# One attention-and-expert kernel, its 850 operations put in another order

## The chip, the cores and the metric

One core of one Trainium2 chip runs the whole program. The metric is the device time of one execution, in microseconds (us). The engines are TensorE (PE; its weight loads are PEld), VectorE (DVE), ScalarE (ACT), GpSimd (POOL) and SyncE (SP). All large transfers here are issued by SP, in the order of its list.

## The reference

The input x is 4 batches of 11,456 rows of 128 floats; there are 32 inducing vectors, a gate of 8 experts, and per expert two matrices (128 x 1024 and 1024 x 128). Cut to what matters:

```
h   = softmax(scale * I @ x.T) @ x             # per batch, 32 rows of 128
y   = softmax(scale * x @ h.T) @ h             # one row per row of x
e   = argmax(y @ w_gate);  g = softmax(y @ w_gate)[e]
out = g * (max(y @ w1[e], 0) @ w2[e])          # the row's own expert
```

Every row of y is a weighted mean of the 32 rows of h. Where all 32 agree on the expert and on the signs of its hidden units, the expert is linear for the whole batch, and out is the row's 32 weights times a 32 x 128 table. The kernel builds that table per batch, checks with margins that it holds for every row, counts the rows for which it does not, and runs a general path for those (none here).

## The kernel before

The 11,456 rows of a batch are cut into 6 pieces, 24 in all (k = 0 to 23; batch b has pieces 6b to 6b+5). A piece is 960 KB. It stays in SBUF from its load to its last use, and there are 19 buffers of that size ("big") for the pieces as loaded, for their transposes, and for the output. So a load has to wait until a buffer is free, and a store frees one.

Each line of `make_plan` is one operation, with a name that the text below uses:

- LT k loads piece k with the 128 features on the partitions. TR k.n turns it on PE and TE k.n evicts the turned part (ACT or DVE); for 10 of the 24 pieces a second load, LN k, brings the turned form instead.
- First pass: S1 k (scores against the inducing vectors, line 680), M1 (maximum, line 683), MQ/FD/NB (maximum over both pieces of a pair), E1 (exponential on ACT, line 720), T1 (transposition on DVE, line 723), H k (weighted sum on PE, line 733), AC.
- Per batch: hT, hn, hc (h, normed and centred), cg and ix (which expert), GA and GB (SP reads the expert's row number, then loads its weights, lines 792 and 793), G, GT, GS, GL, P, PC, PF, h4 (the table), dx to ts (the margins).
- Second pass: S2 k (scores against h, line 680 with hc), M2, N2, E2 (line 915). Four pieces make a round: LG, LV, LS, PR, C, CT compute the gate's factor. Then per piece SP (spread, line 975), W (line 978), four X k.q (line 982), four evictions V k.q (line 699 on ACT, 701 on DVE), and OUT k, the store (line 674).

The same program text, `schedule`, sets the order. It is a planner that runs when the kernel is built: each operation has a rank (a sum of four numbers of `PLAN`), a duration on the engines that may run it, and the operations that it needs. At each moment a free engine takes the ready operation of lowest rank for which a buffer is free. The planner models transfers (`Lines`: rate, restart after a pause), TensorE's row tiles and a price for a change of shape. What comes out is one fixed list per engine; on the chip each engine runs its own list in order, and waits by semaphores. Evictions named in `PLAN["ACT"]` or `PLAN["DVE"]` are bound to that engine; the others go where the planner finds room, and DVE leaves such an eviction to ACT when ACT's list is no more than `BEHIND` ns long.

Of the kernel before, what the change touches and what calls it, by code (L numbers as in the profile page):

```python
# [1324 lines left out]
```

## Time and profile before

| | |
|---|---|
| time, median of 3 runs | 173.77 us (173.07 to 175.04) |
| profiled execution | 174.46 us, its span 172.7 us |
| PE busy | 147.7 us (86% of the span) |
| DVE busy | 132.4 us (77%) |
| ACT busy | 89.8 us (52%) |
| POOL busy | 15.1 us (9%) |
| DMA moved | 61.89 MB, mean 358 GB/s |
| chain that ended last | PE 54%, DMA 30%, DVE 4%, issue 3%, ACT 2% |

Busy time of an engine is the union of its instructions; consecutive DVE and ACT instructions overlap a little in the records, so the sum of durations is larger. A wait is read from the idle time before an instruction and what ended it. Waits on SP are waits of the transfer list: everything behind the waiting transfer waits too.

### The profile page before, as it was taken

The numbers are of one execution on the slowest core, as the hardware profiler recorded it, in microseconds if no ns is written. First come the engines' busy times: TensorE is split into PE (matmuls) and PEld (weight loads), VectorE is DVE, ScalarE is ACT, GpSimd is POOL, SyncE is SP. The second block draws the span as 40 slices with busy tenths as digits, with TensorE's granted clock in tenths as the row PEclk, the third lists the DMA queues.
The fourth block names the chain that finished last, engine by engine and source line by source line (L and its number), as shares of the span: only waits on it lengthen the run. The fifth ranks groups of instructions, "written<-read, shape, count | busy, mean of one in ns | idle before, by whom it ended". The sixth has DMA issues, their size and how long they took to land.

```text
span 172.7 us, 5018 instructions
## 1 busy us (share of the span) xinstructions
PE 147.7 (86%) x1994; PEld 82.0 (48%) x1995; DVE 132.4 (77%) x367; ACT 89.8 (52%) x183; POOL 15.1 (9%) x78
## 2 busy tenths in 40 slices
PE   7799989699999999968998969799999999979000
PEld 4283648585358575637626623135533433325000
DVE  0167978157999899995998969979999999999400
ACT  3141726063674452534086543968397999657000
POOL 0100000000101000220201032000212001120000
PEclk9999999999999999999999999999999999999855
DMA  5999999999999992999995999759767999999991
GB/s 161 419 427 427 422 427 428 416 417 417 413 424 423 388 391 67 390 390 400 352 377 174 331 401 386 234 233 388 294 258 260 390 428 425 420 425 429 418 414 59
DMA packets 9679, 61.89 MB, mean 358 GB/s; under 512 B 1072, under 2 KB 1200, under 8 KB 9648
## 3 DMA queue, kind: packets, MB, share of 16 engines
q1 hardware_dynamic: 9504, 61.29, 88.7%
q8 instruction: 18, 0.29, 0.7%
q10 hardware_dynamic: 144, 0.20, 0.4%
q14 instruction: 13, 0.11, 0.2%
HBM read 37.89 MB, written 23.59 MB: 356 GB/s over the span
## 4 chain that ended last, share of the span: by engine, by line
PE 54%; DMA 30%; DVE 4%; issue 3%; ACT 2%; SPq 0%; DVEq 0%
DMA big<-in_xT 16%; PE bank L680 14%; PE bank L982 12%; PE bank L733 9%; PE bank L691 8%; DMA big<-in_xn 4%; PE bank L975 4%; DMA wt<-in_w 4%; DMA csb<-in_consts 3%; DMA out<-big 3%; DVE big L701 2%; PE bank L919 2%; PE bank L644 2%; ACT big L699 2%; PE bank L820 1%
## 5 line engine op out<-in xcount | busy, mean ns | idle before, releaser
L699 ACT COPY big<-bank 128x480 f32<-128x480 f32 (+2 forms) x110 | 55.2, 574 | 38.6 <-PE bank L691 21.9
L982 PE MATMUL bank<-mid,h 32*128 32x480 f32 x192 | 30.9, 607 | 0.9 <-DVE mid L978 0.7
L701 DVE COPY big<-bank 128x512 f32<-128x512 f32 (+2 forms) x42 | 26.1, 646 | 4.5 <-PE bank L691 4.2
L680 PE MATMUL bank<-big,csb 128*32 128x480 f32 x192 | 24.3, 570 | 4.0 <-DMA big<-in_xT 2.7
L733 PE MATMUL bank<-big,mid 128*32 128x129 f32 x720 | 24.2, 274 | 3.5 <-DMA big<-in_xn 2.2
L691 PE MATMUL bank<-csb,big 128*128 128x128 f32 x210 | 25.9, 277 | 0.4 <-DMA big<-in_xT 0.4
L733 PEld LDWEIGHTS bank<-big,mid 128*32 128x32 f32 x720 | 21.7, 110 | 9.5 <-issue 4.4
L691 PEld LDWEIGHTS bank<-csb,big 128*128 128x128 f32 x210 | 22.6, 141 | 7.2 <-issue 2.2
L683 DVE TENSOR_REDUCE mx<-bank 128x1 f32<-128x480 f32 x24 | 15.5, 647 | 11.7 <-PE bank L680 11.3
L680 PE MATMUL bank<-big,hc 128*32 128x480 f32 x192 | 22.7, 571 | 0.0
L915 ACT ACTIVATE mid<-bank,nb 128x480 f32<-128x480 f32 x24 | 15.8, 676 | 12.5 <-DVE nb L910 10.7
L720 ACT ACTIVATE mid<-bank,mx 128x480 f32<-128x480 f32 x24 | 15.2, 661 | 11.3 <-DVE mx L717 11.1
L982 PEld LDWEIGHTS bank<-mid,h 32*128 32x128 f32 x192 | 12.7, 183 | 14.5 <-ACT big L699 4.7
L906 DVE TENSOR_REDUCE mx<-bank 128x1 f32<-128x480 f32 x24 | 15.2, 639 | 0.5 <-PE bank L680 0.5
L723 DVE STREAM_TRANSPOSE mid<-mid 128x480 f32<-128x480 f32 x24 | 15.5, 660 | 0.0
L978 DVE TENSOR_TENSOR mid<-mid,bank 128x480 f32<-128x480 f32 x24 | 14.8, 639 | 0.6 <-PE bank L975 0.5
L975 PE MATMUL bank<-mid,sel 32*128 32x480 f32 x48 | 14.5, 603 | 0.5 <-DVE mid L971 0.5
L680 PEld LDWEIGHTS bank<-big,csb 128*32 128x32 f32 x192 | 5.8, 109 | 10.5 <-issue 5.9
L680 PEld LDWEIGHTS bank<-big,hc 128*32 128x32 f32 x192 | 5.2, 109 | 8.8 <-ACT big L699 4.3
L975 PEld LDWEIGHTS bank<-mid,sel 32*128 32x128 f32 x48 | 4.6, 183 | 5.1 <-ACT big L699 2.2
L919 PE MATMUL bank<-mid,gzb 128*32 128x480 f32 x48 | 6.0, 574 | 0.0
L902 POOL COPY thr_all<-thr 32x1 f32<-32x1 f32 x24 | 4.3, 177 | 19.5 <-DVE thr L895 18.7
(98 smaller groups left out, 116.6 us busy)
## 6 DMA issues: line engine op xcount, KB each, us to landing
big<-in_xT SPq DMA_DIRECT2D x24, 960.0 KB, 9.3
out<-big SPq DMA_DIRECT2D x24, 960.0 KB, 6.6
big<-in_xn SPq DMA_DIRECT2D x10, 967.5 KB, 9.8
wt<-in_w SPq DMA_DIRECT2D x8, 512.0 KB, 7.1
csb<-in_consts ACTq DMA_DIRECT2D x1, 194.5 KB, 5.8
```

The source lines that it names most:

```text
L680: self.nc.tensor.matmul(self.blk(ps[32 * q : 32 * q + 32, :GW]), lhsT=lhsT, rhs=x[:, :, q, :], start=True, stop=True)
L683: self.nc.vector.tensor_reduce(self.mx1[b][g // 2][:, g % 2 : g % 2 + 1], self.bank(fe)[:, :GW], AX.X, ALU.max)
L691: self.nc.tensor.transpose(ps[:, k * P : (k + 1) * P], x[:, k0 + k].rearrange("p q t -> p (q t)"), self.ident)
L699: self.nc.scalar.copy(dst, src)
L701: self.nc.vector.tensor_copy(dst, src)
L720: self.nc.scalar.activation(self.at(e), self.bank(fe)[:, :GW], AF.Exp, bias=self.mx1[b][p + 1][:, 2:3], scale=SCALE)
L723: self.nc.vector.transpose(self.at(e), self.at(e))
L733: self.nc.tensor.matmul(ps[32 * j : 32 * j + 32, : P + 1], lhsT=e[:, k, :], rhs=x[:, k, :], start=(n < 4), stop=(n >= 2 * GB - 4))
L906: self.nc.vector.tensor_reduce(self.mx2[r][:, u : u + 1], self.bank(fe)[:, :GW], AX.X, ALU.max)
L915: self.nc.scalar.activation(self.at(e), self.bank(fe)[:, :GW], AF.Exp, bias=self.nb2[r][:, u : u + 1])
L975: self.nc.tensor.matmul(self.bank(s)[:, :GW], lhsT=self.sel[rows], rhs=self.at(lv)[rows], start=True, stop=True)
L982: self.nc.tensor.matmul(self.bank(o)[:, :GW], lhsT=self.h4[b][rows], rhs=self.at(e)[rows], start=True, stop=True)
```

## The change

No operation is added or taken away, and the functions that issue instructions are the same. What changes is the planner's input, and with it the four engine lists: the constants for transfers and for a change of shape, the durations of many small operations, the time from a load's end to its use (`LAG`), and all ranks and bound evictions of `PLAN`.

```diff
-HOP, SAME, FREE, RATE, PAUSE, AGAIN, FIRST = 70, 35, 40, 420, 1500, 600, 330000
-SWITCH, STICK, INFLIGHT, BEHIND = 150, 7156, 2, 1821
+HOP, SAME, FREE, RATE, PAUSE, AGAIN, FIRST = 70, 35, 40, 420, 400, 1200, 490000
+SWITCH, STICK, INFLIGHT, BEHIND = 145, 11705, 3, 36141
...
-                    occ, run, lat = occ + SWITCH, run + SWITCH, lat + SWITCH
+                    s = SWITCH - (55 if kind == "F" else 0)
+                    occ, run, lat = occ + s, run + s, lat + s
...
+LAG = 1060
 PLAN = {
     "A": [
-        13444, 10489, 4363, 4657, -1295, -1123, 17739, 6411, 22282, 1339, 15332, -11541, 20566, -9320, -4196, 505,
+        9165, 31839, 23780, 18902, 7067, 7246, 18637, 20028, 35978, 11643, 16022, -5560, 6406, 96, 6396, -6574, 11012,
...
-dma=("SP", BYTES, 7680, 1000, 360))
+dma=("SP", BYTES, 7680, 1000, LAG))
...
-                fd = op(f"FD{b}.{p}", ("A", k, "FD"), pe(200), ...
+                fd = op(f"FD{b}.{p}", ("A", k, "FD"), pe(70, 200), ...
```

Of the 164 evictions, DVE runs 46 before (25 TE, 17 V, 4 small) and 33 with the change (19 TE, 14 V); ACT runs the other 118 and 131. The lines of the new text stand 35 lower than before (680 is 715, 674 is 709, and so on).

Three places in the lists follow. The first is SP's list around the first stores; `big` is a piece's buffer, and L674/L709 are stores, L668/L703 loads of a piece, L671/L706 loads of a turned piece, L792 to L793 and L827 to L828 the fetch of an expert's weights. Before:

```order
L671 DMA big_96<-in_xn 128x1935
L793 ISA
L793 DMA wt_128<-in_w 128x1024
L674 DMA out<-big_101 128x1920
L671 DMA big_87<-in_xn 128x1935
L668 DMA big_101<-in_xT 128x1920
L674 DMA out<-big_93 128x1920
```

With the change:

```order
L828 DMA wt_128<-in_w 128x1024
L706 DMA big_92<-in_xn 128x1935
L706 DMA big_87<-in_xn 128x1935
L828 ISA
L828 DMA wt_128<-in_w 128x1024
L709 DMA out<-big_86 128x1920
L709 DMA out<-big_90 128x1920
L709 DMA out<-big_92 128x1920
```

Before, the last piece (LT22) is loaded into the buffer that the first store (OUT3) frees, `big_101`, and S1 of that piece waits for both. Now all 34 loads of x stand ahead of the first store.

The second place is PE's list where the second pass over batch 1 begins (`hc_184` is the centred h of batch 1; L680/L715 with it is S2, L691/L726 a turn, L919/L954 the logits, L975/L1010 a spread). Before, twelve groups of turns stand between the logits of round 0 and this score, the last six of them here:

```order
L691 MATMUL bank_79<-csb,big_85 128x128 x4
L691 MATMUL bank_83<-csb,big_91 128x128 x4
L691 MATMUL bank_77<-csb,big_91 128x128 x4
L691 MATMUL bank_80<-csb,big_86 128x128 x3
L691 MATMUL bank_81<-csb,big_91 128x128 x3
L691 MATMUL bank_82<-csb,big_85 128x128 x4
L820 MATMUL bank_77<-wt_128,hT_all 32x256 x4
L680 MATMUL bank_83<-big_94,csb 32x480 x4
L680 MATMUL bank_80<-big_102,hc_184 32x480 x4
```

With the change:

```order
L954 MATMUL bank_78<-mid_119,gzb_195 32x480
L715 MATMUL bank_84<-big_102,hc_184 32x480 x4
L715 MATMUL bank_83<-big_94,hc_184 32x480 x4
L715 MATMUL bank_82<-big_90,hc_184 32x480 x4
L679 MATMUL bank_80<-csb,hs_208 32x8 x4
```

Three scores of batch 1 now follow the logits of round 0 at once, and with each of them a buffer is done with; the turns of batch 2 come behind.

The third place is DVE's list from the centred h of batch 2 on (`hc_185`; L683/L718 is M1, L906/L941 is M2, L723/L758 is T1, L861, L862 and L896, L897 are dx, L894 is th, L1000 and L1001 are in C). Before:

```order
L771 TENSOR_SCALAR hc_185<-hT_all,hs_209 128x32
L894 TENSOR_REDUCE thr_200<-bank_83 128x1
L895 TENSOR_SCALAR thr_200<-thr_200 128x1
L906 TENSOR_REDUCE mx_1_172<-bank_84 128x1
L683 TENSOR_REDUCE mx_3_2_143<-bank_78 128x1
L781 TENSOR_REDUCE sm_2_217<-bank_80 128x1
```

With the change:

```order
L806 TENSOR_SCALAR hc_185<-hT_all,hs_209 128x32
L896 TENSOR_REDUCE u_1_229<-gT_225 128x8
L897 TENSOR_REDUCE u_1_229<-gT_225 128x8
L758 STREAM_TRANSPOSE mid_108<-mid_108 128x480
L907 RECIPROCAL u_1_229<-u_1_229 128x16
L1000 TENSOR_REDUCE se_124<-mid_117 128x60
L1001 SCALAR_TENSOR_TENSOR se_124<-se_124,sm_122 128x60
```

From this row to the end DVE has 155 rows before and 144 with the change: four W, one LV with its LS, one each of M1, M2, N2, MQ, NB, T1, PC and one V fewer, one set of margins (dx, di, dm) and one th more.

## Rows read from the trace of the kernel before

**Rows 1.** Page, part 2: what the transfers moved, 40 slices of the span.
```profile
GB/s 161 419 427 427 422 427 428 416 417 417 413 424 423 388 391 67 390 390 400 352 377 174 331 401 386 234 233 388 294 258 260 390 428 425 420 425 429 418 414 59
```

**Rows 2.** Windows: length, busy of PE, PEld, DVE, ACT, POOL, clock, DMA share, GB/s.
```profile
2.70:60.00 57.30, 53.08 (x790) 34.45 (x792) 39.50 (x98) 24.70 (x47) 2.55 (x18) 1.00 1.01 417
60.00:72.00 12.00, 12.00 (x199) 8.60 (x188) 11.75 (x35) 5.63 (x12) 1.28 (x5) 1.00 0.72 271
72.00:85.00 13.00, 10.81 (x220) 7.72 (x222) 10.66 (x30) 4.06 (x8) 1.46 (x8) 1.00 1.00 388
85.00:95.00 10.00, 9.38 (x161) 4.79 (x154) 8.93 (x27) 6.61 (x15) 1.38 (x7) 1.00 0.77 283
95.00:135.00 40.00, 37.26 (x470) 15.42 (x469) 35.43 (x109) 27.29 (x58) 5.89 (x25) 1.00 0.81 310
135.00:168.80 33.80, 23.52 (x182) 10.04 (x174) 25.91 (x64) 20.05 (x43) 2.17 (x10) 0.91 1.01 418
```

**Rows 3.** Waits of SP's list, 60 to 140 us: total, times, longest.
```profile
SPq L668 <- PE bank L680: 14.7, 4, 9.8
```

**Rows 4.** Timeline of SP: start, duration, transfers issued.
```profile
66.95 3.02 SPq L668 DMA_DIRECT2D big<-in_xT  x2
...
158.49 3.31 SPq L674 DMA_DIRECT2D out<-big  x3
```

**Rows 5.** Chain that ended last, 84 to 115 us: start, duration, what.
```profile
88.84 5.52 DMA out<-big
...
94.38 7.99 DMA big<-in_xT
```

**Rows 6.** Waits of PE, whole span.
```profile
PE bank L680 <- DMA big<-in_xT: 2.7, 4, 1.4
PE bank L733 <- DMA big<-in_xn: 2.2, 1, 2.2
```

**Rows 7.** Timeline of PE, 96 to 114 us: the score of the last piece.
```profile
102.51 1.01 PE L680 MATMUL bank<-big,csb 128*32 128x480 f32 x8 [1.43 <-DMA big<-in_xT]
```

**Rows 8.** Chain, whole span: pieces of PE work (30 records of L733 are one H).
```profile
51.86 0.81 PE bank L680 x8
...
61.17 3.52 PE bank L691 x29
...
82.63 0.76 PE bank L733 x27
```

**Rows 9.** Windows: from hc of batch 2 to DVE's last eviction.
```profile
101.20:161.20 60.00, 54.31 (x532) 22.20 (x532) 54.85 (x151) 43.03 (x91) 7.55 (x33) 1.00 0.88 356
```

**Rows 10.** Timeline of DVE: start, duration, count, idle before it.
```profile
103.65 0.66 DVE L683 TENSOR_REDUCE mx<-bank 128x1 f32<-128x480 f32 x1 [1.50 <-PE bank L680]
...
153.82 2.35 DVE L978 TENSOR_TENSOR mid<-mid,bank 128x480 f32<-128x480 f32 x4 [0.25 <-PE bank L975]
156.09 5.16 DVE L701 COPY big<-bank 128x480 f32<-128x480 f32 x9
```

**Rows 11.** Groups by line: count, busy us, mean ns, idle before.
```profile
L699 ACT COPY big<-bank 128x480 f32<-128x480 f32 x79 | 39.1, 578 | 16.2 <-PE bank L982 15.0 <-ACT big L699 0.9
...
L683 DVE TENSOR_REDUCE mx<-bank 128x1 f32<-128x480 f32 x24 | 15.5, 647 | 11.7 <-PE bank L680 11.3
...
L924 DVE STREAM_TRANSPOSE mid<-bank 128x480 f32<-128x480 f32 x6 | 4.0, 673 | 0.2
...
L947 DVE CUSTOM_DVE_ANT_1 mid<-mid,rs 128x420 f32<-128x420 f32 x6 | 3.6, 596 | 0.2
...
L946 DVE RECIPROCAL rs<-sm 128x60 f32<-128x60 f32 x6 | 3.2, 528 | 0.2
...
L861 DVE TENSOR_REDUCE u<-gT 128x8 f32<-128x256 f32 x4 | 1.6, 401 | 0.0
```

**Rows 12.** Waits of ACT for DVE: total, times, longest.
```profile
ACT mid L720 <- DVE mx L717: 11.1, 7, 3.2
ACT mid L915 <- DVE nb L910: 10.7, 7, 3.0
```

More of the change, by code (lines that the diff above doesn't have):

```diff
@@ L437, in make_plan @@
             fe = Buf("fe")
-            ld = op(f"LT{k}", ("L", k, ""), {"SP": (400, 400)}, lambda xt=xt, b=b, g=g: K.load_xt(xt, b, g), take=[xt], dma=("SP", BYTES, 7680, 1000, 360))
+            ld = op(f"LT{k}", ("L", k, ""), {"SP": (400, 400)}, lambda xt=xt, b=b, g=g: K.load_xt(xt, b, g), take=[xt], dma=("SP", BYTES, 7680, 1000, LAG))
             s1[g] = op(f"S1.{k}", ("A", k, "S1"), pe(800), lambda fe=fe, xt=xt: K.scores(fe, K.it_s, xt), [ld, warm], take=[fe], use=[xt], kind="C")
@@ L449, in make_plan @@
             else:
-                xr = [op(f"LN{k}", ("N", k, ""), {"SP": (400, 400)}, lambda xn=xn[g], b=b, g=g: K.load_xn(xn, b, g), take=[xn[g]], dma=("SP", 990720, 7740, 1000, 360))]
+                xr = [op(f"LN{k}", ("N", k, ""), {"SP": (400, 400)}, lambda xn=xn[g], b=b, g=g: K.load_xn(xn, b, g), take=[xn[g]], dma=("SP", 990720, 7740, 1000, LAG))]
             e1[g] = (fe, Buf("e1"), xr)
@@ L454, in make_plan @@
                 hp = Buf("mi")
[L455 to L457 removed]
+                mq = op(f"MQ{b}.{p}", ("A", k, "MQ"), vec(60), lambda b=b, p=p: K.max_spread(b, p), [m1[g - 1], m1[g], nb_prev])
+                fd = op(f"FD{b}.{p}", ("A", k, "FD"), pe(70, 200), lambda fe=fe, b=b, p=p: K.max_fold(fe, b, p), [mq], use=[fe], kind="C")
+                nb = op(f"NB{b}.{p}", ("A", k, "NB"), vec(78), lambda fe=fe, b=b, p=p: K.max_all(fe, b, p), [fd], use=[fe])
                 hs = []
@@ L465, in make_plan @@
                         last = op(f"ZP{ku}", ("A", ku, "ZP"), {"POOL": (60, 130)}, lambda e=e1_: K.zero_pad(e), [tt], use=[e1_])
-                    hs.append(op(f"H{ku}", ("A", ku, "H"), pe(830), lambda hp=hp, e=e1_, xn=xn[u], u=u: K.h_sum(hp, e, xn, u), [last, *xr_, *hs], take=[hp] if u == g - 1 else [], use=[hp, e1_, xn[u]], kind="C"))
+                    hs.append(op(f"H{ku}", ("A", ku, "H"), pe(815, 830), lambda hp=hp, e=e1_, xn=xn[u], u=u: K.h_sum(hp, e, xn, u), [last, *xr_, *hs], take=[hp] if u == g - 1 else [], use=[hp, e1_, xn[u]], kind="C"))
                 f = None
@@ L469, in make_plan @@
                     f = op(f"F{b}.{p}", ("A", k, "F"), {"ACT": (185, 300)}, lambda b=b, p=p: K.factor(b, p), [nb])
-                acc = op(f"AC{b}.{p}", ("A", k, "AC"), vec(240), lambda hp=hp, b=b, p=p: K.h_acc(hp, b, p), [hs[1], f, acc], use=[hp])
+                acc = op(f"AC{b}.{p}", ("A", k, "AC"), vec(260), lambda hp=hp, b=b, p=p: K.h_acc(hp, b, p), [hs[1], f, acc], use=[hp])
                 nb_prev = nb
         m0 = Buf("mi")
-        a = op(f"hT{b}", ("C", b, "hT"), pe(450), lambda mi=m0, b=b: K.h_turn(mi, b), [acc], take=[m0], kind="C")
-        a = hT = op(f"hn{b}", ("C", b, "hn"), vec(910), lambda mi=m0, b=b: K.h_norm(mi, b), [a], use=[m0])
-        a = hc = op(f"hc{b}", ("C", b, "hc"), vec(380), lambda b=b: K.h_center(b), [a])
+        a = op(f"hT{b}", ("C", b, "hT"), pe(310, 450), lambda mi=m0, b=b: K.h_turn(mi, b), [acc], take=[m0], kind="C")
+        a = hT = op(f"hn{b}", ("C", b, "hn"), vec(820), lambda mi=m0, b=b: K.h_norm(mi, b), [a], use=[m0])
+        a = hc = op(f"hc{b}", ("C", b, "hc"), vec(330), lambda b=b: K.h_center(b), [a])
         m0 = Buf("mi")
-        a = op(f"cg{b}", ("C", b, "cg"), pe(400), lambda mi=m0, b=b: K.gate_mm(mi, b), [hc], take=[m0], kind="C")
+        a = op(f"cg{b}", ("C", b, "cg"), pe(140, 300), lambda mi=m0, b=b: K.gate_mm(mi, b), [hc], take=[m0], kind="C")
         a = ix = op(f"ix{b}", ("C", b, "ix"), vec(740), lambda mi=m0, b=b: K.pick(mi, b), [a], use=[m0])
-        cc = op(f"cc{b}", ("C", b, "gt"), {"ACT": (185, 290), "DVE": (150, 240)}, lambda e, mi=m0, b=b: K.gate_out(e, mi, b), [a], use=[m0])
+        cc = op(f"cc{b}", ("C", b, "gt"), {"ACT": (165, 270), "DVE": (60, 140)}, lambda e, mi=m0, b=b: K.gate_out(e, mi, b), [a], use=[m0])
         w = Buf("w")
@@ L484, in make_plan @@
         else:
-            ga = op(f"GA{b}", ("C", b, "GA"), {"SP": (2000, 2000)}, lambda w=w, b=b: K.fetch("SP", w, b, 0, F), [ix], take=[w], dma=("SP", 524288, 4096, 2600, 600))
-            gc = op(f"GB{b}", ("C", b, "GA"), {"SP": (450, 450)}, lambda w=w, b=b: K.fetch("SP", w, b, F, 2 * F), [ga], use=[w], dma=("SP", 524288, 4096, 1000, 600))
+            ga = op(f"GA{b}", ("C", b, "GA"), {"SP": (2000, 2000)}, lambda w=w, b=b: K.fetch("SP", w, b, 0, F), [ix], take=[w], dma=("SP", 524288, 4096, 2600, LAG))
+            gc = op(f"GB{b}", ("C", b, "GA"), {"SP": (450, 450)}, lambda w=w, b=b: K.fetch("SP", w, b, F, 2 * F), [ga], use=[w], dma=("SP", 524288, 4096, 1000, LAG))
         gz = op(f"gt{b}", ("C", b, "gt"), {"POOL": (550, 600)}, lambda b=b: K.gate_turn(b), [ix, cc])
-        gz = op(f"gz{b}", ("C", b, "gz"), vec(280), lambda b=b: K.gate_cols(b), [gz])
+        gz = op(f"gz{b}", ("C", b, "gz"), vec(360), lambda b=b: K.gate_cols(b), [gz])
         gzb = op(f"gb{b}", ("C", b, "gb"), {"POOL": (250, 330)}, lambda b=b: K.gate_block(b), [gz])
@@ L491, in make_plan @@
         a = op(f"G{b}", ("C", b, "G"), pe(430), lambda mi=m0, w=w, b=b: K.units(mi, w, b), [ga, hT], take=[m0], use=[w], kind="C")
-        gt = op(f"GT{b}", ("C", b, "GT"), vec(450), lambda mi=m0, b=b: K.units_turn(mi, b), [a, *marks[-2:-1]], use=[m0])
-        gs = op(f"GS{b}", ("C", b, "GS"), vec(420), lambda b=b: K.units_sum(b), [gt])
-        gl = op(f"GL{b}", ("C", b, "GL"), vec(590), lambda b=b: K.units_keep(b), [gs])
+        gt = op(f"GT{b}", ("C", b, "GT"), vec(365), lambda mi=m0, b=b: K.units_turn(mi, b), [a, *marks[-2:-1]], use=[m0])
+        gs = op(f"GS{b}", ("C", b, "GS"), vec(325), lambda b=b: K.units_sum(b), [gt])
+        gl = op(f"GL{b}", ("C", b, "GL"), vec(545), lambda b=b: K.units_keep(b), [gs])
         m0 = Buf("mi")
@@ L498, in make_plan @@
         m0 = Buf("mi")
-        a = op(f"PF{b}", ("C", b, "PF"), pe(300), lambda mi=m0, b=b: K.part_fold(mi, b), [a], take=[m0], kind="C")
+        a = op(f"PF{b}", ("C", b, "PF"), pe(220, 300), lambda mi=m0, b=b: K.part_fold(mi, b), [a], take=[m0], kind="C")
         h4 = op(f"h4{b}", ("C", b, "h4"), {"ACT": (165, 270), "DVE": (200, 280)}, lambda e, mi=m0, b=b: K.h4_out(e, mi, b), [a], use=[m0])
-        a = op(f"dx{b}", ("C", b, "dx"), vec(720), lambda b=b: K.extremes(b), [gl])
+        a = op(f"dx{b}", ("C", b, "dx"), vec(655), lambda b=b: K.extremes(b), [gl])
         marks.append(a)
         a = op(f"dg{b}", ("C", b, "dg"), {"POOL": (260, 300)}, lambda b=b: K.guards(b), [a])
-        a = op(f"di{b}", ("C", b, "di"), vec(120), lambda b=b: K.inverses(b), [a])
+        a = op(f"di{b}", ("C", b, "di"), vec(155), lambda b=b: K.inverses(b), [a])
         a = op(f"dr{b}", ("C", b, "dr"), {"POOL": (130, 180)}, lambda b=b: K.ratios(b), [a])
-        a = op(f"dm{b}", ("C", b, "dm"), vec(160), lambda b=b: K.margin(b), [a])
+        a = op(f"dm{b}", ("C", b, "dm"), vec(250), lambda b=b: K.margin(b), [a])
         a = op(f"dd{b}", ("C", b, "dd"), {"POOL": (350, 400)}, lambda b=b: K.diagonal(b), [a])
         m0 = Buf("mi")
-        a = op(f"DF{b}", ("C", b, "DF"), pe(300), lambda mi=m0, b=b: K.margin_all(mi, b), [a], take=[m0], kind="C")
+        a = op(f"DF{b}", ("C", b, "DF"), pe(225, 300), lambda mi=m0, b=b: K.margin_all(mi, b), [a], take=[m0], kind="C")
         th = op(f"th{b}", ("C", b, "th"), vec(360), lambda mi=m0, b=b: K.threshold(mi, b), [a], use=[m0])
@@ L532, in make_plan @@
         lgo = op(f"LG{r}", ("R", r, "LG"), pe(800), lambda lg=lg, e2=e2, bs=bs: K.logits(lg, e2, bs), [*exs, *[gzs[b] for b in bs]], take=[lg], use=[lg, *e2], kind="C")
-        lt = op(f"LV{r}", ("R", r, "LV"), vec(640), lambda lg=lg, lv=lv, n=n: K.logits_turn(lg, lv, n), [lgo], take=[lv], use=[lg])
-        ls = op(f"LS{r}", ("R", r, "LS"), vec(250, 520, 560), lambda lv=lv, gate=gate, n=n, r=r: K.gate_ls(lv, gate, n, r), [lt], take=[gate], use=[lv])
+        lt = op(f"LV{r}", ("R", r, "LV"), vec(610), lambda lg=lg, lv=lv, n=n: K.logits_turn(lg, lv, n), [lgo], take=[lv], use=[lg])
+        ls = op(f"LS{r}", ("R", r, "LS"), vec(255, 530, 580), lambda lv=lv, gate=gate, n=n, r=r: K.gate_ls(lv, gate, n, r), [lt], take=[gate], use=[lv])
         pr = op(f"PR{r}", ("R", r, "PR"), {"ACT": (460, 570)}, lambda lv=lv, n=n: K.gate_exp(lv, n), [ls], use=[lv])
-        c = op(f"C{r}", ("R", r, "C"), vec(600, 250, 530), lambda lv=lv, gate=gate, n=n: K.gate_c(lv, gate, n), [pr], use=[lv, gate])
+        c = op(f"C{r}", ("R", r, "C"), vec(570, 220, 530), lambda lv=lv, gate=gate, n=n: K.gate_c(lv, gate, n), [pr], use=[lv, gate])
         cb = op(f"CT{r}", ("R", r, "CT"), vec(590), lambda lv=lv, gate=gate, n=n: K.turn_c(lv, gate, n), [c], use=[lv, gate])
@@ L546, in make_plan @@
                 vs.append(op(f"V{k}.{q}", ("X", k, "V"), {"ACT": act(480), "DVE": dve(480)}, lambda e, o=os_[q], ob=ob, q=q: K.evict(e, o, ob, q), [x], use=[os_[q], ob]))
-            op(f"OUT{k}", ("X", k, "OUT"), {"SP": (400, 400)}, lambda ob=ob, b=b, g=k % NG: K.store(ob, b, g), vs, use=[ob], dma=("SP", BYTES, 7680, 1000, 360))
+            op(f"OUT{k}", ("X", k, "OUT"), {"SP": (400, 400)}, lambda ob=ob, b=b, g=k % NG: K.store(ob, b, g), vs, use=[ob], dma=("SP", BYTES, 7680, 1000, LAG))
     m0 = Buf("mi")
```

27 lines of the change are left out of this document (12 added, 15 removed), and 253 rows, old and new, of the table PLAN.

## The prediction

> **What bounds the kernel now.** First the slices of what the transfers move [rows 1]: they reach 427 GB/s and stay there up to slice 13, then fall into holes, and are full again from slice 33 to 39. 61.89 MB at 427 GB/s are 144.9 us, so 27.8 us of the 172.7 us span are not transfer. Next the windows [rows 2] say where. A window's loss is its length times (1 - its GB/s / 427): 1.3 us from 2.7 to 60, 4.4 from 60 to 72, 1.2 to 85, 3.4 to 95, 11.0 to 135, 0.7 to 168.8. That is 22.0; the other 5.8 us are the start, and the 3.9 us from 168.8 to the end.
>
> Then who makes the holes. In the first, SP's list waits for a score on PE, up to 9.8 us at a time [rows 3], and the load is issued at 66.95 [rows 4]; the buffer it waits for belongs to a piece whose second-pass score stands late in PE's list. The second hole is a chain [rows 5]: store OUT3 at 88.84 lands after 5.52 us, the load into its buffer needs 7.99 more, and the score of that piece starts at 102.51, PE having idled for 1.43 us [rows 7] and DVE for 1.50 [rows 10]. The third hole, 95 to 135, is different: but for the end of that load only weights and stores are left, and a store waits until its piece is computed. There PE is busy 37.3 of 40 us and DVE 35.4 [rows 2]. So the start is bound by transfers, the middle by PE with buffers behind it, and from 95 us on by PE and DVE together; the last 33.8 us are transfers again (418 GB/s), working off stores that queued up: the last ones are issued from 158.49 on [rows 4], 7 us before the transfers are through.
>
> The consequence for the sum: the end moves by as much as compute moves up in the third hole, provided that the first two holes shrink, so that the transfers are not themselves late when they come there.
>
> **The change, part by part.** The work is the same, PE's sum with it. Three things move.
>
> *DVE's list.* Between the centred h of batch 2 and DVE's last eviction lie 60.0 us, of which DVE is busy 54.85 and PE 54.31 [rows 9]. Behind the same row the new list has four W fewer at 2.35/4 = 0.59 us each (2.35), one V at 5.16/9 = 0.57 [rows 10], one LV (0.67) with its LS (0.53 and 0.60), and one each of M1, M2 and T1 at about 0.65 (1.95, priced by M1); one dx more costs 2 x 0.40 [rows 11]. Sum: 2.35 + 0.57 + 0.67 + 1.13 + 1.95 - 0.80 = 5.9 us. The small ones left out on both sides (MQ, NB, N2, PC against di, dm, th) are below 1 us each way. Eleven of the 13 evictions that leave DVE sit further ahead, where the loads or PE set the pace (PE 12.0 of 12.0 us, DVE 39.5 of 57.3 [rows 2]): those I cost at nothing; if DVE set the pace there too, they would add 11 x 0.57 = 6.3.
>
> *PE's list up to the same point.* Ahead of hT of batch 2 stand 36 scores instead of 33, 3 logits instead of 2, 21 H instead of 22, and 20 row-tiled products (SP and X) in both. A score takes 0.81, logits are priced like one, an H 0.76 x 30/27 = 0.84 [rows 8]: 3 x 0.81 + 0.81 - 0.84 = 2.4 us later. Against it stand the waits ahead of that point: 2.2 us for a turned piece and 2.7 - 1.4 = 1.3 us for three others [rows 6]. The turned piece that PE waited for (LN17) is loaded with more room, and the early loads come in an order in which PE has something left to do. I take both waits as gone: 1.1 us gained. The bounds are 1.1 gained and 2.4 lost, should new waits of that size come.
>
> *SP's list.* All loads of x now stand ahead of the first store. The chain store, load, score is gone, with the 1.5 us that DVE idled [rows 10]. In its place the first store waits for four evictions with nothing else queued. The first hole goes with the batch 1 scores that now follow the logits of round 0 at once. What is late next is the load of the last turned piece, which needs the buffer of H 15; I leave 1.0 of the 4.4 us and 1.5 of the 3.4 us standing. New risk sits further ahead: five loads (LN19 to LT16) now wait for the first scores of the second pass. Ahead of the first of these PE does 13 first scores instead of 11, 150 turns instead of 120 and 10 H instead of 8: 2 x 0.81 + 30 x 3.52/29 + 2 x 0.84 = 6.9 us more [rows 8]. How much slack those loads had the trace does not tell; the cost lies between 0 and 6.9, and I take 1.7, near the low end, since the transfers ran full there [rows 2].
>
> A page speaks against the SP term. The Trainium skill, DMA: Bandwidth & Descriptors, Anatomy of one DMA, fits a transfer at 2.0 us plus its bytes at 436 GB/s, 4.3 us for a piece; the store and the load would then be over by 97.3, no score would have waited, and the sum would be 5.2 instead of 6.7. The measured 5.52 and 7.99 us [rows 5] decide.
>
> *ACT* gets 13 x 0.578 = 7.5 us [rows 11]; it has 17 us free in the last 60 [rows 9]. Costed at nothing while that holds.
>
> **The sum.** If DVE sets the pace after 101 us: 1.1 + 1.5 + 5.9 = 8.5 us. If PE does: only waits that go count, 2.2 + 1.3 + 1.4 = 4.9 us. DVE's 54.85 and PE's 54.31 are as good as equal, so I take the middle, 6.7. The transfers allow it: losses of 1.3 + 1.7, 1.0, 1.2, 1.5 and 0.7 leave 22.0 - 6.7 - 7.4 = 7.9 us for the third hole, which now has 11.0. The profiled execution took 174.46 us, 0.69 above the median of the three, with 1.76 around its span: it would become 167.8. From the median 173.77 the time is 167.1 us.
>
> **The rivals.** *PE sets the pace throughout.* Then 4.9 us are gained: 168.9. For it: PE is busy 12.0 of 12.0 us from 60 to 72 and its work is unchanged [rows 2]. Against: in the last stretches PE's records are stretched by waiting for banks to be evicted, and DVE is as full. Chance 0.28, with times from 168 to 172.
>
> *The holes move forward.* The five loads lose the whole 6.9 us instead of 1.7, and everything behind them is as much later: 167.1 + 5.2 = 172.3, no change. For it: the later first scores, certain from the list. Against: the transfers are late by all of it only if they had no slack at all, and up to 60 us they lost 1.3 us in all [rows 2]. Chance 0.14.
>
> *ACT becomes the brake, and the kernel slower.* ACT runs its list in order. Its exponentials wait for DVE 14 times in the trace, 21.8 us in all, 1.56 each [rows 12]. An eviction that stood on DVE and now stands behind such a wait keeps its bank, and PE with it. With n of the 13 so placed the time changes by 1.56 n - 6.7: slower by over 1% from n = 6 on, 178.0 with 7, 187 with all. Against: 15.0 of the 16.2 us that ACT idled ahead of its 480-wide evictions ended with PE [rows 11], so ACT waits for PE and not the other way round. Chance 0.11.
>
> **How the numbers follow.** The forecast (165 to 168.5) has 0.47, the rivals 0.28, 0.14 and 0.11. About 1% of 173.77, 1.74 us, is what a measurement of this kernel can tell from no change. Faster takes the forecast, the first rival and a little of the second: 0.77. Within 1%: 0.13. Slower: 0.10. Low end of the range: DVE's 8.5 and the 2.4 us by which PE's list behind hT of batch 2 is shorter, 163.0 rounded up. High end: the middle of the second rival's times, 173.0. Outside lie the third rival, the upper half of the second and a few per cent below.
>
> **What would show it.** Right: the rate between 60 and 95 us holds above 380 GB/s; SP waits for L715 (the old L680) for under 7 us between 60 and 140; no load stands behind a store; DVE's last eviction ends near 154 us instead of 161; the stores are again queued at the end. DVE at least 91% busy behind hc of batch 2 says that DVE sets the pace, and a PE busy share well above DVE's that PE does. Wrong: a rate under 400 GB/s before 60 us (second rival); L734 evictions on ACT, or PE's weight loads behind them, idling for ACT's exponentials for more than 8 us in all (third rival). A clock below 1.00 before the last store, which no window but the last shows now [rows 2], would make all of it wrong.

## The result, and the profile after

The changed kernel takes 166.03 us (median of 4 runs, 165.42 to 166.97) against 174.29 us (4 runs, 173.07 to 175.04): a ratio of 0.954, with a 95% interval from 0.946 to 0.962. The forecast was 167.1 us. The profiled execution took 165.42 us with a span of 163.6; the sum of the prediction, made against 174.46 us, would have put it at 167.8. Some executions run at a lower granted clock and take some per cent longer; they count in no ratio below, and of two kernels (the one with more work on PE, and the one with two scores behind turns) only such an execution was profiled, so no row of theirs is used.

First the slices of what the transfers moved, from the page, as in [rows 1].

```profile
GB/s 164 427 428 426 419 426 430 417 416 420 343 339 351 423 417 375 426 431 407 420 402 310 256 418 269 279 399 412 380 372 378 427 421 423 428 424 423 419 359 28
```

The hole of 67 GB/s in the sixteenth slice is gone. Three shallower ones have come in the eleventh to thirteenth, where there were none, and the slices from 400 GB/s down in the middle are fewer and less deep. The windows, to be held against [rows 2] (length, busy of PE, PEld, DVE, ACT, POOL, clock, DMA share, GB/s):

```profile
2.70:60.00 57.30, 56.24 (x834) 37.25 (x836) 40.54 (x102) 25.27 (x51) 2.62 (x18) 1.00 0.99 405
60.00:72.00 12.00, 11.43 (x164) 6.83 (x156) 10.41 (x30) 7.41 (x16) 1.14 (x4) 1.00 1.01 406
72.00:85.00 13.00, 12.85 (x221) 7.48 (x217) 12.16 (x37) 7.29 (x16) 1.23 (x5) 1.00 1.02 413
85.00:95.00 10.00, 9.05 (x167) 6.19 (x167) 9.67 (x27) 8.26 (x19) 0.12 (x1) 1.00 0.86 306
95.00:135.00 40.00, 39.90 (x542) 20.39 (x537) 37.88 (x118) 33.09 (x72) 7.57 (x33) 1.00 0.96 374
135.00:159.70 24.70, 11.94 (x92) 6.17 (x84) 14.58 (x37) 10.73 (x23) 2.18 (x10) 0.82 0.99 411
```

By the prediction's rule (length times 1 - GB/s / 427) the losses are 2.95, 0.6, 0.4, 2.8, 5.0 and 0.9 us, 12.7 in all, where 22.0 were lost before and 15.3 were forecast. The span became 9.1 us shorter, and 9.3 us of lost transfer time went.

Two rows of the timeline of DVE give the split of the compute side (start, duration, count, idle before it): the centred h of batch 2, and the last evictions.

```profile
98.06 0.24 DVE L806 TENSOR_SCALAR hc<-hT_all,hs 128x32 f32<-128x32 f32 x1
...
149.59 1.21 DVE L736 COPY big<-bank 128x480 f32<-128x480 f32 x2
```

Before, the first of these ended at 101.2 and the last eviction at 161.25 [rows 9, 10]. So the front comes 2.9 us earlier, the stretch behind it is 52.5 us instead of 60.1 (7.6 us shorter), and from the last eviction to the end of the span pass 12.8 us instead of 11.45 (1.35 us given back): 2.9 + 7.6 - 1.35 = 9.1.

In the stretch from 98.3 to 150.8 us the windows give, in the same columns:

```profile
98.30:150.80 52.50, 48.53 (x526) 23.66 (x518) 49.78 (x143) 42.73 (x91) 9.62 (x42) 1.00 0.98 387
```

DVE is busy 95% of it, PE 92%, ACT 81%; in [rows 9] it was 91, 91 and 72%.

Last the waits, of SP's list from 60 to 140 us and of ACT (total, times, longest):

```profile
SPq L709 <- ACT big L734: 25.9, 13, 5.7
SPq L703 <- PE bank L715: 11.2, 4, 5.1
```

```profile
ACT mid L950 <- DVE nb L945: 6.4, 7, 2.1
...
ACT mid L755 <- DVE mx L752: 3.2, 3, 2.1
```

A load still waits for a score four times, but for 5.1 us at most instead of 9.8 [rows 3]. ACT's exponentials wait for DVE for 9.6 us in all instead of 21.8 [rows 12].

### The profile page after: what moved, and what is told of

It reads as the page before. It is cut to its first block, busy times and chain, and to the rows that moved or that the text cites. A ratio compares the mean times of both kernels' runs of the same rounds, so it can differ in the third digit from the quotient of the medians.

```text
span 163.6 us, 5024 instructions
## 1 busy us (share of the span) xinstructions
PE 143.0 (87%) x1994; PEld 85.3 (52%) x1995; DVE 125.5 (77%) x354; ACT 93.5 (57%) x196; POOL 15.2 (9%) x78
## 4 chain that ended last, share of the span: by engine, by line
PE 74%; DMA 8%; DVE 5%; ACT 3%; issue 2%; DVEq 0%; SPq 0%
PE bank L715 25%; PE bank L726 15%; PE bank L768 11%; PE bank L1017 10%; DMA wt<-in_w 5%; PE bank L1010 4%; DMA csb<-in_consts 3%; PE bank L679 3%; PE bank L954 3%; ACT big L734 3%; DVE big L736 2%; PE bank L877 1%; DVE mid L1013 1%; PE bank L855 1%; DVE mx L941 0%
## 5 line engine op out<-in xcount | busy, mean ns | idle before, releaser
L734 ACT COPY big<-bank 128x480 f32<-128x480 f32 (+2 forms) x119 | 58.4, 590 | 30.9 <-PE bank L726 22.9
L1017 PE MATMUL bank<-mid,h 32*128 32x480 f32 x192 | 31.9, 596 | 0.7 <-ACT h L734 0.6
L715 PE MATMUL bank<-big,csb 128*32 128x480 f32 x192 | 25.7, 598 | 1.8 <-DMA csb<-in_consts 1.1
L726 PE MATMUL bank<-csb,big 128*128 128x128 f32 x210 | 26.1, 280 | 0.0
L726 PEld LDWEIGHTS bank<-csb,big 128*128 128x128 f32 x210 | 23.3, 143 | 5.3 <-issue 3.7
L718 DVE TENSOR_REDUCE mx<-bank 128x1 f32<-128x480 f32 x24 | 15.6, 651 | 11.4 <-PE bank L715 9.6
L736 DVE COPY big<-bank 128x480 f32<-128x480 f32 (+2 forms) x33 | 19.9, 637 | 3.9 <-PE bank L726 3.7
L715 PE MATMUL bank<-big,hc 128*32 128x480 f32 x192 | 22.2, 569 | 0.0
L1017 PEld LDWEIGHTS bank<-mid,h 32*128 32x128 f32 x192 | 15.8, 183 | 10.8 <-ACT big L734 4.2
L758 DVE STREAM_TRANSPOSE mid<-mid 128x480 f32<-128x480 f32 x24 | 15.6, 662 | 0.3
L941 DVE TENSOR_REDUCE mx<-bank 128x1 f32<-128x480 f32 x24 | 15.2, 642 | 0.3
L1010 PE MATMUL bank<-mid,sel 32*128 32x480 f32 x48 | 14.5, 599 | 0.8 <-ACT big L734 0.8
L715 PEld LDWEIGHTS bank<-big,hc 128*32 128x32 f32 x192 | 5.7, 110 | 10.4 <-issue 4.6
L715 PEld LDWEIGHTS bank<-big,csb 128*32 128x32 f32 x192 | 5.6, 112 | 8.7 <-issue 2.8
L1010 PEld LDWEIGHTS bank<-mid,sel 32*128 32x128 f32 x48 | 4.9, 183 | 3.5 <-ACT big L734 2.5
L954 PE MATMUL bank<-mid,gzb 128*32 128x480 f32 x48 | 6.0, 569 | 0.0
L721 POOL MEMSET big<- 128x15 f32 x14 | 1.4, 123 | 48.1 <-PE bank L768 30.8
```

The costliest lines, as they stand in the source:

```text
L715: self.nc.tensor.matmul(self.blk(ps[32 * q : 32 * q + 32, :GW]), lhsT=lhsT, rhs=x[:, :, q, :], start=True, stop=True)
L718: self.nc.vector.tensor_reduce(self.mx1[b][g // 2][:, g % 2 : g % 2 + 1], self.bank(fe)[:, :GW], AX.X, ALU.max)
L726: self.nc.tensor.transpose(ps[:, k * P : (k + 1) * P], x[:, k0 + k].rearrange("p q t -> p (q t)"), self.ident)
L734: self.nc.scalar.copy(dst, src)
L736: self.nc.vector.tensor_copy(dst, src)
L758: self.nc.vector.transpose(self.at(e), self.at(e))
```

## The experiments

Each kernel ran beside the kernel before on one chip, and its ratio to it is what is compared; the kernel before itself had medians of 173.8, 175.1 and 175.6 us in the three groups. Microseconds are (ratio - 0.954) x 174, good to about 2 us where the interval is no wider than the changed kernel's. Times of single rows are of one execution each; two kernels below whose lists do not differ up to batch 2's h have it at 98.06 and 99.12, so such times are good to about 1 us.

### Order or engines?

**The new order, the old engines.** Each eviction is issued on the engine that ran it before:

```diff
-            if len(o.dur) > 1:
-                o.fn(o.eng)
+            if o.raw:
+                o.raw("DVE" if o.name in ON_DVE else "ACT")
```

> The new order of all operations, but each of the 164 evictions on the engine that ran it before: DVE has 46 of them again instead of 33, 10 of the 13 more ahead of hc of batch 2 and 3 behind it. An eviction on DVE took 0.57 us. DVE theory (DVE's list sets the pace behind hc of batch 2, the transfers and PE ahead of it): 3 x 0.57 = 1.7 us more than the changed kernel's 166.0, 167.7; if DVE sets the pace ahead of it too, 13 x 0.57 = 7.4 us, 173.4. PE theory (PE's list sets the pace throughout): 166.0, within 1 us. Transfer theory (the gain came from the place of loads, stores and batch 1 scores): 166.0 as well, and 0 of the gain lies in the choice of engines. A time at or above 173 would say that the gain is the choice of engines and not the order.

169.5 us, ratio 0.974 (0.969 to 0.980): 3.5 us lost. DVE's centred h of batch 2 and its last evictions:

```profile
101.36 0.24 DVE L814 TENSOR_SCALAR hc<-hT_all,hs 128x32 f32<-128x32 f32 x1
...
156.32 1.21 DVE L744 COPY big<-bank 128x480 f32<-128x480 f32 x2
```

The first starts at 101.36 instead of 98.06, and the last eviction ends at 157.5 instead of 150.8. So the engines are worth 3.5 us. On DVE's side half of the delay arises ahead of batch 2's h, which is 3.3 us later, and half behind it (55.9 us instead of 52.5); the end of the span is 4.3 us later (167.9 instead of 163.6), so the queue of stores absorbs a part.

**The old order, the new engines**, by the same edit in the old kernel.

> The order from before, but each eviction on the engine that the changed kernel gives it: DVE has 33 instead of 46, 11 fewer ahead of hc of batch 2 and 2 fewer behind. DVE theory: DVE behind hc of batch 2 has 2 x 0.57 = 1.1 us less, and the store, load, score chain is still there: 174.3 - 1.1 = 173.2. PE theory and transfer theory: no gain, 174.3 within 1 us. If the choice of engines is what the change brings: 167 to 169. If evictions put on ACT without their order being searched for it stand behind exponentials there: slower, 175 to 180.

175.8 us, ratio 1.009 (1.002 to 1.017): no gain, rather a loss. The centred h of batch 2 starts at 100.77 instead of 100.94:

```profile
100.77 0.24 DVE L778 TENSOR_SCALAR hc<-hT_all,hs 128x32 f32<-128x32 f32 x1
```

The choice of engines that is worth 3.5 us in the new order is worth nothing in the old one; the order alone brings 2.6%, both together 4.6%.

**The new order, the old engines early alone**: DVE has 29 evictions ahead of the centred h of batch 2 instead of 19, and one more behind it; the other late ones are as changed.

> The changed kernel with the engines from before for the evictions ahead of hc of batch 2 alone: 30 of them on DVE instead of 19 (turns, three small ones, and one eviction each of output pieces 2 and 3), and the 14 late ones of the output on DVE as the changed kernel has them. All 13 at once had cost 169.5 - 166.0 = 3.5 us, where the prediction held that the early ones are free. If the early ones are free: 166.0 within 1 us, and the 3 late ones cost the 3.5. If DVE's list sets the pace early as well: 11 x 0.57 = 6.3 us at most, and 3 us (what all 13 cost, less 3 x 0.57 late) is the likely amount: 168 to 170, with the first store later by that much.

168.2 us, ratio 0.965 (0.957 to 0.972): 1.9 us lost, which is no more than the margin of such a difference. Windows of the changed kernel, and then of this one (columns as above):

```profile
60.00:75.00 15.00, 14.28 (x192) 7.83 (x188) 13.18 (x37) 8.69 (x18) 1.14 (x4) 1.00 1.00 406
75.00:90.00 15.00, 15.00 (x323) 10.04 (x315) 14.25 (x44) 9.27 (x23) 1.35 (x6) 1.00 0.98 385
```

```profile
60.00:75.00 15.00, 14.85 (x196) 7.81 (x199) 14.69 (x39) 6.79 (x13) 1.14 (x4) 1.00 1.00 403
75.00:90.00 15.00, 13.43 (x247) 7.63 (x243) 14.79 (x46) 6.99 (x14) 1.32 (x6) 1.00 0.89 341
```

DVE has 29.5 of 30 us full, PE does 247 products instead of 323 in the second window, the transfers lose 44 GB/s, and the h of batch 2 comes later:

```profile
100.59 0.24 DVE L814 TENSOR_SCALAR hc<-hT_all,hs 128x32 f32<-128x32 f32 x1
```

That is 2.5 us later than in the changed kernel. The kernel with less work on DVE, further down, is a second measure: up to this point its list is the changed kernel's, and it was measured in the same group as this one. It does 284 products in the second window and has the h at 99.12, so the delay is 1.5 us against it.

```profile
75.00:90.00 15.00, 14.70 (x284) 9.12 (x283) 13.79 (x42) 9.85 (x22) 1.35 (x6) 1.00 0.96 369
```

In the old order, with all 30 early evictions on DVE, the same two windows are:

```profile
60.00:75.00 15.00, 15.00 (x239) 9.80 (x231) 14.72 (x42) 6.04 (x12) 1.37 (x5) 1.00 0.77 296
75.00:90.00 15.00, 12.81 (x239) 8.34 (x232) 12.45 (x36) 6.81 (x14) 2.05 (x10) 1.00 0.97 375
```

There DVE was as full up to 75 us, but had 2.5 of 15 us free behind it.

### DVE or PE?

**More work on DVE.** Twelve reduces for which nobody waits:

```diff
+            if o.name in MORE:                      # M2.12 to M2.23
+                K.nc.vector.tensor_reduce(K.cnt, K.csb[:, 0:384], AX.X, ALU.max)
```

> The changed kernel with 12 more reduces on DVE (128 x 384 of a constant into a scratch column, one behind each second-pass maximum M2 of pieces 12 to 23), for which nobody waits; about 0.5 us each, 6 us of DVE work, all behind hc of batch 1 and nearly all behind hc of batch 2. DVE theory: 5 to 6 us more, 171 to 172, and DVE's last eviction later by as much. PE theory: DVE had 2.1 us free of 40 between 95 and 135 us and more later; 0 to 2 us more, 166 to 168. Transfer theory: 0 to 1 us.

169.0 us, ratio 0.976 (0.968 to 0.983): 3.8 us lost by 12 x 0.542 = 6.5 us of work. A window of it, and its last evictions:

```profile
95.00:135.00 40.00, 40.00 (x484) 19.98 (x475) 38.50 (x120) 29.36 (x63) 7.52 (x33) 0.98 0.88 342
```

```profile
154.77 1.21 DVE L738 COPY big<-bank 128x480 f32<-128x480 f32 x2
```

Its h of batch 2 ends at 97.9, so the stretch behind it is 58.1 us, 5.6 more: nearly all of what is added to DVE's list comes back in it, and the last eviction is 5.2 us later; with a span of 167.2 us the end is 3.6 later, and the queue of stores absorbs the other 1.6. A part may be the clock's: over this stretch the granted clock is 0.97, with some 3.4 us at 0.50 around 135 us, where the changed kernel has 1.00. The two kernels with old engines on the new order have 0.97 there too. What of their losses is the clock's, no run separates.

```profile
97.90:155.98 58.08, 54.16 (x526) 25.80 (x518) 55.00 (x155) 42.96 (x91) 9.56 (x42) 0.97 0.91 361
```

The other thing to see is PE: busy for 40.00 of 40 us, fuller than in the changed kernel, with 484 products instead of 542. No PE work was added. Up to 130 us, where the clock is 1.00 in both, the windows and the products X of the changed kernel and then of this one are:

```profile
95.00:130.00 35.00, 34.97 (x495) 18.26 (x489) 32.95 (x106) 28.61 (x63) 7.57 (x33) 1.00 0.96 368
L1017 PE MATMUL bank<-mid,h 32*128 32x480 f32 x95 | 15.8, 599 | 0.0
```

```profile
95.00:130.00 35.00, 35.00 (x464) 17.40 (x456) 33.64 (x106) 24.95 (x54) 7.52 (x33) 1.00 0.90 345
L1019 PE MATMUL bank<-mid,h 32*128 32x480 f32 x80 | 15.7, 600 | 0.0
```

One record is as long in both, 0.60 us, so the records do not show a waiting product as a longer one. What changes is how many run side by side: 95 x 0.599 us in 15.8 us are 3.6 at a time, 80 x 0.600 in 15.7 are 3.1. Busy time is a union, and it counts a moment with one product as it counts one with four.

**More work on PE.** Seven second-pass scores are done twice, by `o.fn()` once more for S2.12 to S2.18.

> The changed kernel with 7 second-pass scores (pieces 12 to 18) multiplied twice into the same banks: 7 x 0.81 = 5.7 us more of PE work at most, with the same results, and nothing more on any other engine. PE theory: 5 to 6 us more, 171 to 172. DVE theory: PE's records behind hc of batch 2 are stretched by waiting for banks, so that most of the added work goes into those waits; 0 to 2 us more, 166 to 168, though the 7 maxima that wait for a doubled score come up to 0.81 us later each. If both engines share the pace, as PE 39.90 and DVE 37.88 of 40 us between 95 and 135 us may also mean: both this kernel and the one with more DVE work lose 2 to 5 us.

169.9 us, ratio 0.976 (0.970 to 0.982): 3.9 us lost by at most 5.7 us of work. The PE theory wanted 5 to 6, the DVE theory 0 to 2; what came is nearest to the third case, that both engines lose, though the margin of 2 us reaches the edges of the other two.

**Less work on DVE.** Six late evictions go to ACT.

> The changed kernel with 6 of the 14 late output evictions (V8.3, V12.1, V14.0, V16.1, V17.1, V19.3) moved from DVE to ACT, in the same order: 6 x 0.57 = 3.4 us less for DVE behind hc of batch 2, 3.5 us more for ACT, which is busy 33.1 of 40 us between 95 and 135 us. If DVE's list alone sets the pace there: 3 us less, 163. If PE's does: 166.0 within 1 us. If all three are full in turn (12 more reduces cost 3.0 of their 6.5 us, 7 more scores 3.9 of 5.7), what DVE gains ACT loses, and the evictions on ACT stand behind its exponentials: 166 to 169.

166.9 us, ratio 0.952 (0.945 to 0.959): no change. DVE has 3.4 us less to do, and yet its last eviction comes later, and the stretch from batch 2's h to it is 54.1 us instead of 52.5:

```profile
99.12 0.24 DVE L812 TENSOR_SCALAR hc<-hT_all,hs 128x32 f32<-128x32 f32 x1
...
152.21 1.21 DVE L742 COPY big<-bank 128x480 f32<-128x480 f32 x2
```

The waits of DVE, of this kernel, say where it went:

```profile
DVE mid L1019 <- PE bank L1016: 3.0, 4, 1.3
DVE se L1006 <- ACT mid L1001: 2.2, 2, 1.5
```

In the changed kernel the first of these pairs is 1.7 us and the second does not occur. What is taken from DVE it idles away, waiting for PE and ACT. Work added to either engine costs 60 to 70% of itself; work handed from DVE to ACT gives nothing. What DVE would gain if ACT did not get the work, this run does not show.

**The same two additions to the kernel before.**

> The kernel before with the same 12 reduces on DVE (0.54 us each, 6.5 us in all) that cost the changed kernel 2.2% or 3.8 us. Behind hc of batch 2 DVE and PE were as good as equally busy there, 54.85 and 54.31 of 60 us. If DVE's list set the end before: 4 to 6 us more. If the transfer holes did (the chain store, load, score, and the weights): DVE has slack while they last, 0 to 2 us more. If PE and DVE shared the pace: about 3 us.

> The kernel before with the same 7 second-pass scores (pieces 12 to 18) twice, 5.7 us of PE work, which cost the changed kernel 2.3% or 3.9 us. If PE's list set the end before: 4 to 6 us more. If DVE's did or the holes: 0 to 2 us. If they shared the pace: about 3 us.

177.9 us, ratio 1.021 (0.993 to 1.048), and 179.1 us, ratio 1.031 (1.014 to 1.047). The interval of the first takes in all its theories. The second is 5.3 us (2.5 to 8.2): the old kernel had no free room on PE either, and more it does not say.

### The transfer list

**A load behind a store.** The load of piece 22 stands behind the first store in SP's list again, and the score S1.22 behind the two:

```diff
-        for o in schedule(make_plan(K, PLAN), CAPS, GROUPS):
+        for o in later(schedule(make_plan(K, PLAN), CAPS, GROUPS), {"LT22": "OUT0"}):
```

> The changed kernel with one load moved: that of piece 22 stands behind the first store again and so does its first-pass score (5 places later in PE's list); the chain store, load, score is back. Chain theory (the prediction's 1.5 us): the load is issued at about 90 us instead of about 80 and lands near 100, PE and DVE idle for 1.5 to 4 us, 167.5 to 170. Compute theory (from 95 us on the engines, not the transfers, are late): the load fills the hole between 85 and 95 us, PE has other work meanwhile, and the time stays 166.0 within 1 us.

180.3 us, ratio 1.033 (1.025 to 1.040): 13.7 us lost, where 1.5 to 4 had been expected of the chain. It is not quite the old chain. There the load took the buffer that the store had to free; here its buffer is another, which the changed kernel fills from 70.80 on, and the load is issued 0.42 us behind the store without waiting for it to land. What is late is the issue itself, at 88.31. Timelines of SP and of PE:

```profile
87.89 0.38 SPq L738 DMA_DIRECT2D out<-big  x1
88.31 0.52 SPq L732 DMA_DIRECT2D big<-in_xT  x1
```

```profile
86.75 1.01 PE L983 MATMUL bank<-mid,gzb 128*32 128x480 f32 x8
99.15 1.83 PE L744 MATMUL bank<-big,csb 128*32 128x480 f32 x8 [11.38 <-DMA big<-in_xT]
```

In the old list some 12 us of PE work stand between the store at 88.84 and the score of the last piece at 102.51 [rows 5, 7], so that PE waited 1.4 us for the chain. In this one PE is through with all that stands ahead of the score at 87.76, before the store is issued at 87.89, and idles until the load has landed. What PE waits for such a load is not the length of the transfers but that length less the work that the list puts ahead of the score.

**The same, with the score ten places further back** (`"S1.22": "SP8"` added to the table). Two H, five X and three spreads now stand ahead of it; three operations that stood among them (FD3.2, SP11 and X2.1) fall behind it.

> The kernel with the load of piece 22 behind the first store, which took 180.25 us (ratio 1.033 to before) with PE idle for 11.4 us ahead of that piece's score; here the score stands 12 places further back in PE's list, behind 2 H, 5 X, 3 spreads and the partial product, which took from 88.25 to about 93 us in the changed kernel. Distance theory (a chain costs its length less the work that the list puts between load and score): PE idles for about 11.4 - 5 = 6.4 us, and the time falls by 5 us: ratio 1.004, about 175. If the chain's cost is the late load itself (store queue, batch 3 late): no change, 1.033. If the idle time had cost more than its length, because the clock fell to 0.58 from 90 to 102 us: more than 5 us back, below 1.00.

180.0 us, ratio 1.039 (1.017 to 1.061). The wait fell to 6.3 us, as the distance theory had it, but the time did not fall with it. Windows of the kernel with the load behind the store, and then of this one:

```profile
92.00:96.00 4.00, 0.00 (x0) 0.00 (x0) 0.00 (x0) 0.00 (x0) 0.00 (x0) 0.50 0.99 368
...
100.00:104.00 4.00, 4.00 (x84) 2.72 (x76) 2.92 (x8) 0.53 (x2) 0.00 (x0) 0.74 0.00 0
104.00:108.00 4.00, 4.00 (x54) 2.62 (x50) 3.90 (x13) 4.00 (x10) 0.00 (x0) 1.00 0.02 4
```

```profile
98.99 1.83 PE L745 MATMUL bank<-big,csb 128*32 128x480 f32 x8 [6.31 <-DMA big<-in_xT]
```

```profile
100.00:104.00 4.00, 1.84 (x18) 0.87 (x14) 1.00 (x3) 1.62 (x4) 0.00 (x0) 0.50 0.01 4
104.00:108.00 4.00, 4.00 (x26) 2.11 (x28) 2.54 (x8) 2.40 (x6) 0.00 (x0) 0.50 0.00 0
108.00:112.00 4.00, 4.00 (x86) 3.82 (x81) 2.08 (x7) 0.83 (x3) 0.12 (x1) 0.50 0.97 399
112.00:116.00 4.00, 4.00 (x66) 1.61 (x62) 3.53 (x13) 2.73 (x7) 0.70 (x3) 1.00 0.24 96
```

In the first kernel the work that had piled up keeps PE full from 100 us on, and the clock is back at 1.00 by 104. In the second that work was done earlier; what follows the late score are steps that wait for each other, and the clock stays at 0.50 until 112 us. So the distance theory holds for the wait and fails for the time. The work behind the score and the clock are what differs; how the loss divides between these two, no run here separates.

**Two scores of batch 1 behind the turns of piece 14 again** (`{"S2.11": "TR14.0", "S2.9": "TR14.0"}` in the same edit).

> The changed kernel with two of the three batch 1 scores that follow the logits of round 0 (pieces 9 and 11) moved behind the turns of piece 14, as they stood before; the loads that need their buffers stand later in the transfer list too. Transfer theory (the hole between 60 and 72 us closed because those scores free buffers early): the rate from 60 to 72 us falls from 406 towards 271 GB/s, and 1 to 4 us are lost, 167 to 170. If the hole's closing was worth nothing, since the loads behind it had slack: the hole comes back and the time stays 166.0 within 1 us.

172.9 us, the median of four runs from 170.5 to 177.8; the ratio, from two of them, is 0.981 (0.970 to 0.991): 4.7 us lost, above the 1 to 4 of the transfer theory but within 2 us of them. So the place of these scores is worth something; whether it is the hole at 60 to 72 us that came back is not shown.

**The weights ahead of a load.** In the changed kernel PE has one wait on a transfer left between 60 and 100 us, for the second half of an expert's weights (timeline of PE), which is issued behind two loads of turned pieces (timeline of SP):

```profile
94.85 0.65 PE L877 MATMUL bank<-wt,gl 128*32 128x128 f32 x16 [0.94 <-DMA wt<-in_w]
```

```profile
80.08 6.78 SPq L706 DMA_DIRECT2D big<-in_xn  x2
87.12 1.34 SPq L828 DMA_DIRECT2D wt<-in_w  x1
88.51 13.07 SPq L709 DMA_DIRECT2D out<-big  x4
```

The edit is `{"LN20": "GB1"}`: the fetch goes between the two.

> The changed kernel with the second half of the weights of batch 1's expert fetched ahead of the load of the last turned piece, instead of behind it. PE waited 0.94 us for those weights, which landed 7.6 us behind their issue at 87.1, with that load just ahead of them. If that wait is on the path: 0.5 to 1 us less, 165.0 to 165.5 (ratio 0.949). If not, or if the turned piece and the first stores are late by as much instead: 166.0 within 1 us.

164.2 us (163.27 to 165.00), ratio 0.948 (0.932 to 0.963). The timeline of SP:

```profile
80.45 0.35 SPq L858 DMA_DIRECT2D wt<-in_w  x1
85.86 0.33 SPq L736 DMA_DIRECT2D big<-in_xn  x1
86.71 13.20 SPq L739 DMA_DIRECT2D out<-big  x4
```

The weights are issued 6.7 us earlier, PE's wait is gone, the h of batch 2 comes 1.3 us earlier (little more than such times are good to) and the first store 1.8. It is the fastest kernel of the study, and all its four runs lie below all four of the changed kernel; but the two did not run side by side, and the interval of its ratio takes in the other's. That it is faster is likely and not shown.

## Why the prediction was right, point by point

- **What bounds it, and the holes.** Right in the sum, less so in the places. The holes were to shrink from 22.0 to 15.3 us, and shrank to 12.7. The early risk (1.7 us taken of 0 to 6.9) is there with its size: 2.95 us are lost up to 60 us, forecast 3.0, and SP's list waits for a score for 4.9 us at once between 43 and 48 us. The hole from 85 to 95 us was left at 1.5 and measures 2.8; the third was left at 7.9 and measures 5.0.
- **DVE's list behind batch 2's h.** Right in its sum: 5.9 + 1.5 = 7.4 us were forecast, the stretch is 7.6 us shorter. The parts are less exact: DVE's busy time there fell by 5.1 us (54.85 to 49.78) instead of 5.9, its idle time by 2.4 instead of 1.5. That the stretch came through whole decides against the middle that the sum took: the DVE reading, 8.5 us, was the nearer one to 9.1. How near it came is in part luck, since the front gave 1.8 us more than forecast and the stores took 1.35 that no term had. The run with more DVE work shows that DVE's list is a limit of this stretch (5.6 of 6.5 us, with the clock in it); that it is the only one is not shown, since 3.4 us less work on it did not shorten the stretch.
- **PE's list ahead of it, 1.1 us gained.** Too small: 2.9. The step that failed is the one that costed the early evictions at nothing. On the old order that is so (0.2 us by the run with new engines alone); in the new one, with these evictions, DVE has 29.5 of 30 us full, and there they are worth 1.5 to 2.5 us of the front. That leaves 0.4 to 1.4 us to the order itself. The term was read from the slack of the old order, which the change uses up.
- **The chain store, load, score.** Its 1.5 us were sized from the old list; they are part of the 7.6, and no run took the chain alone out of that list. In the new list a load put back behind the store costs 13.7 us, though it does not even wait for the store to land. The fit that the prediction quotes from the Trainium skill, DMA: Bandwidth & Descriptors, Anatomy of one DMA, is given there for transfers that GpSimd issues. All of these are issued by SP, and whether it would hold for one of them alone, no run here shows.
- **ACT at nothing.** Right as far as is shown: its exponentials wait for less than before. Six more evictions on it, taken from DVE, change nothing in sum, which does not say that they are free.
- **The rivals.** *PE sets the pace throughout* (168.9): not as told, for 9.1 us were gained and not 4.9; but 5.7 us more PE work do cost 3.9, so PE is no free engine either. What spoke against it in the prediction, records of PE stretched by waiting, was misread: at a clock of 1.00 one X took 0.60 us in the changed kernel and in the one with more DVE work, and 0.60 in the kernel before as well (68 records from 95 to 130 us). PE can be busy and yet run fewer products side by side. *Holes move forward*: they did, by the 1.7 us in the sum, not by 6.9. *ACT*: no sign of it.
- **What is missing from the sum**: the stores. The last eviction comes 10.45 us earlier, the end 9.1; the queue of stores keeps 1.35.
- **The signs.** Those of DVE's last eviction (near 154; 150.8), of the stores and of the clock came as told. The rate between 60 and 95 us held only up to 85; SP's waits for scores came to 11.2 us, not under 7, though the hole at 60 to 72 us went. The sign for PE, a busy share well above DVE's, was a bad one: PE's share between 95 and 135 us is 39.90 of 40 and is 40.00 with fewer products, when DVE is loaded.

The Trainium skill, Perfetto Trace Analysis, Identifying the Most-Contended Engine, calls the busy share of matmuls not a good measure of how close a kernel is to roofline; it names instead the matmul FLOPs done, as a share of the peak, and the busy share of weight loads. This case's trace agrees on the first, with 35.00 us for 464 products against 34.97 for 495. On weight loads it agrees where the clock is 1.00 in both, from 95 to 130 us: they fall from 18.26 to 17.40 us, 5%, where the products fall by 6%. Over 95 to 135 us, a part of it at the lower clock, they fall by 2% only (20.39 to 19.98) and the products by 11%.

## What to carry to other kernels

Cost an instruction that leaves an engine by the slack of the new order, not of the old: the same early evictions were worth 0.2 us of the front in one list and 1.5 to 2.5 in the other. Price the wait behind a late transfer by its length less the work that the list puts ahead of its consumer, but do not take the wait for the loss: with 5 us less of it the time stayed the same here. Don't read a full PE as the limit: add work to one engine at a time and see whose list grows. Work that is moved from one engine to another tests both at once.

## What the runs showed of the hardware

In the 11.4 us without PE work the granted clock fell to 0.50, which is 1.2 GHz, and the first score behind them took 1.83 us, where the same eight products took 1.01 [rows 7]. After a shorter pause, 6.3 us, the first score took 1.83 us as well, and the clock stayed at 0.50 for longer, until 112 instead of 104 us. In that time PE was busy 1.84 of 4 us, and then did 26 and 86 products in 4 us each; behind the longer pause it did 84 in the first 4 us. That a shorter wait can cost as much as a longer one was not expected.

PE's busy time does not tell how many products run side by side: 95 and 80 products X, each 0.60 us long, filled 15.8 and 15.7 us.
